# Queries from 256 on: decay rows fetched two heads ahead into five zeroed buffers, not one head ahead into three

## The chip, the cores and the metric

One core of a Trainium2 chip runs the whole program. The metric is the device time of one execution in microseconds (us); lower is better. Engines are called TensorE (PE; its weight loads are PEld), VectorE (DVE), ScalarE (ACT), GpSimd (POOL) and SyncE (SP). SP issues nearly all transfers here, in the order of its queue.

## What is computed

A causal attention with per-step decay, then two MLP blocks. Four batches, eight heads, 576 positions, 64 channels per head. Only the attention's scores matter for the change:

```python
scores = scale * np.matmul(q, k.transpose(0, 1, 3, 2))
cum = np.cumsum(np.log(np.clip(f, 0.0001, 1.0)), axis=-1)
decay = cum[:, :, :, None] - cum[:, :, None, :]
scores = np.where(causal, -1000000000.0, scores + decay)
attn = softmax(scores)            # row maximum taken off first, 1e-9 in the sum
out = np.matmul(attn, v)
x = out of all heads side by side
x = x + relu(layernorm(x) * g @ w_ch1) @ w_ch2
...                               # then a gated MLP with a mix over positions
```

The decay is a difference of two sums, one of the query's position and one of the key's, so four extra rows under a head's 64 channels (sum and one, each in a high and a low part) let the score matmul add it.

## The kernel before

The positions of a batch are worked on in three kinds of blocks: the first 128, the next 128, and the queries from 256 on (320 of them, `QW`). Beside the attention blocks run the token blocks of the first MLP (`mlp`, L808): its two products, L858 into `ph` and L843 into `acc`, are most of TensorE's work and alternate with the attention's matmuls. ScalarE makes `hh` (L869) and VectorE `hl` (L873) from `ph`.

The change is in the third kind, `attention` (L567), which runs once per batch, so 32 heads in all. It goes over four pairs of heads. For each head `operands` (L325) builds the two matmul operands: the key and query columns come by a DMA into `qk` (L330); ScalarE rounds them into `x1` and the queries' upper part into `x2` (both through `copy`, L319); VectorE writes the rounding remainders (L341 into `x1`, L342 into `x2`). Rows 64 to 67 of `x2` hold the four decay rows, which a DMA of SP brings from `decay_d` in device memory (L338); the other rows from 64 on must be zero, so the `x2` tiles are not taken from a rotating pool but are three fixed tiles (`x2z`), zeroed once by GpSimd (L335) and used in turn. `qk` and `x1` have three buffers each as well (`BUFS`, L29).

`weights` (L345) then makes scores of one query block: a matmul with `x2` and one with `x1` (L359), masking with a row minimum on VectorE (L363), exponential on ScalarE (L367), probabilities in two halves (L319 and L380), and a transpose by DMA (L382). Query blocks 2 and 3 are done head by head, block 4 for both heads of a pair together, so that the `x1` and `x2` tiles of both heads of a pair come free when block 4's matmuls are done. `operands` of a head is written one head before that head's `weights`.

The order on each engine and queue is not the order of the text. The program's scheduler runs a model of the chip at compile time and puts an instruction into its engine's queue when the model finds it ready; among ready ones, what was written earlier goes first, except where an order is written out (`after`, `in_order`; the transposes among themselves are). On the chip each queue then runs in that fixed order, and an instruction that waits holds up those behind it.

After its attention a block is stored (L1343), normalised in place (`norm`, L754; the centring is L776) and handed to the MLP.

Of the kernel before, what the change touches and what calls it, by code (L numbers as in the profile page):

```python
# [7 lines left out]
F32R = mybir.dt.float32r  # L8
# [10 lines left out]
P = 128  # L19
B, H, S, D = 4, 8, 576, 64  # L20
# [5 lines left out]
TOK = 256  # L26
QW = S - 2 * P
SC = 2.0 ** 14
BUFS = dict(vr=1, vp=2, qk=3, x1=3, x2=3, PT=4, sd=3, st=6, P16=5, xt=1)  # L29
BUFS0 = dict(vr=1, qk=1, e=4, diag=2, PT=2, st=4)  # L30
BUFS1B = dict(vr=4, vp=4, qk=4, sd=4, P16=4, PT=3, st=8)
BUFS1 = dict(vr=3, vp=3, qk=3, sd=2, P16=2, PT=2, st=6)
# [43 lines left out]
def qtile(i):  # L76
    return i * P, min(S, (i + 1) * P)


def f32(ap):  # L80
    return ap.bitcast(F32)
# [7 lines left out]
class Kernel:  # L89
# [227 lines left out]
    def copy(self, e, out, in_, scale=1.0):  # L317
# [4 lines left out]
        else:  # L322
            self.nc.vector.tensor_scalar(out=out, in0=in_, scalar1=scale, scalar2=None, op0=ALU.mult)

    def operands(self, bh):  # L325

        nc, at = self.nc, self.at
        W, C = QW, QW + S
        qk = at.tile([P, C], F32, tag="qk", name="qk", bufs=BUFS["qk"])
        nc.sync.dma_start(out=qk, in_=self.qk[bh // H, bh % H])  # L330
        x1 = at.tile([P, C], F32R, tag="x1", name="x1", bufs=BUFS["x1"])
        if not self.x2z:
            for i in range(BUFS["x2"]):
                self.x2z.append(at.tile([P, C], F32R, name=f"x2z{i}"))
                nc.gpsimd.memset(f32(self.x2z[i][64:]), 0.0)  # L335
        x2 = self.x2z[0]
        self.x2z.append(self.x2z.pop(0))
        nc.sync.dma_start(out=f32(x2[64:68]), in_=self.decay_d[:, bh // (2 * H) * 2 * H + bh % H * 2 + bh // H % 2])  # L338
        self.copy(0, x1, qk)
        self.copy(0, x2[:64, :W], qk[:64, :W])  # L340
        nc.vector.tensor_tensor(out=x1[64:, :W], in0=qk[64:, :W], in1=f32(x1[64:, :W]), op=ALU.subtract)  # L341
        nc.vector.tensor_tensor(out=x2[:64, W:], in0=qk[:64, W:], in1=f32(x1[:64, W:]), op=ALU.subtract)  # L342
        return [(x[:, :W], x[:, W:]) for x in (x2, x1)]

    def weights(self, i, heads):  # L345

        nc, at, bufs, q0 = self.nc, self.at, BUFS, 2 * P
        lo, hi = qtile(i)
# [218 lines left out]
    def attention(self, b, xT, xt):  # L567
        nc, at, bufs = self.nc, self.at, BUFS
        q0, W = 2 * P, QW
        stored = xt is None  # L570
        if stored:
            xt = at.tile([P, NP, S - 512], F32, tag="xt", name="xt", bufs=bufs["xt"])

        def values(p, vp, vsc, heads, behind=None):

            pav = self.bank("av")
            for kt in range(5):
                n0 = max(kt * P, q0) - q0
                for vi, pi in ((0, 1), (1, 0), (0, 0)):
                    for u in range(2):  # L580
                        us = slice(64 * u, 64 * u + 64)
                        ins = nc.tensor.matmul(  # L582
                            pav[us, n0:W], lhsT=vp[:, vi, kt, us], rhs=heads[u][1][:, 2 * kt + pi, n0:W],
                            start=(kt == 0 and (vi, pi) == (0, 1)), stop=(kt == 4 and (vi, pi) == (0, 0)), skip_group_check=True)
                        if behind is not None and kt == 0 and (vi, pi) == (0, 1):
                            self.after(ins, behind)
            nc.scalar.activation(xT[:, p, :], pav[:, :TOK], AF.Copy, scale=vsc)
            nc.scalar.activation(xt[:, p, :], pav[:, TOK:W], AF.Copy, scale=vsc)
            if p == 1:
                self.xs = self.mo_sum(xT)  # L590
            elif p == 2:
                nc.vector.tensor_tensor(out=self.xs, in0=self.xs, in1=xT[:, 2, :], op=ALU.add)

        late = None
        passes = self.operands(b * H)
        for p in range(NP):
            heads = []
            for u in range(2):
                heads.append((passes, at.tile([P, 10, W], F16, tag="PT", name="PT", bufs=bufs["PT"])))
                if 2 * p + u + 1 < H:  # L600
                    passes = self.operands(b * H + 2 * p + u + 1)
                if u:
                    vr = at.tile([P, 5, P], F32, tag="vr", name="vr", bufs=bufs["vr"])
                    nc.sync.dma_start(out=vr, in_=self.v[b, :, p * P : (p + 1) * P].rearrange("(t p) d -> p t d", p=P))
                yield
                for i in (2, 3):
                    done = self.weights(i, heads[u:])
                    if late and (u, i) == (1, 2):
                        yield
                        values(*late, done)  # L610
                    yield
            vp = at.tile([P, 2, 5, P], F16, tag="vp", name="vp", bufs=bufs["vp"])
            self.weights(4, heads)
            vsc = self.parts16(vr, vp[:, 0], vp[:, 1], b)
            late = p, vp, vsc, heads
            yield
        yield
        values(*late)
        yield
        if stored:  # L620
            nc.sync.dma_start(out=self.xt_d[:, :, b, :], in_=xt)
        return self.xs
# [907 lines left out]
```

## Time and profile before

| | us |
|---|---|
| three runs | 769.38, 771.96, 771.42 |
| median | 771.42 |
| the profiled execution | 774.42 |
| its span, first to last instruction | 772.6 |

Rows are of that one profiled execution. Times start with the span's first instruction. In a list of instructions the columns are start, duration, engine, line, operation, what is written and read, shapes and count; in brackets stands how long the engine was idle before, and what ended it. SPq is SP's queue of transfers.

### The profile page before, as it was taken

How to read it: one execution, taken by the hardware profiler on the slowest of the kernel's cores; microseconds unless marked ns; L12 is line 12 of the kernel's file. 1: busy time of each engine (PE TensorE's matmuls, PEld its weight loads, DVE VectorE, ACT ScalarE, POOL GpSimd, SP SyncE). 2: the span in 40 equal slices, each digit the busy share in tenths (PEclk: the TensorE clock that was granted, in tenths of full speed). 3: DMA queues.
4: the chain of work that ended last, by engine and by line, in shares of the span. 5: the costliest groups of instructions: out<-in, count | busy, mean ns of one | idle time of the engine just before them, and what ended most of it. 6: DMA issues, size and time to landing. Idle time of an engine off the chain costs nothing.

```text
span 772.6 us, 16271 instructions
## 1 busy us (share of the span) xinstructions
PE 747.0 (97%) x5924; PEld 573.0 (74%) x5924; DVE 584.9 (76%) x1549; ACT 528.1 (68%) x1318; POOL 67.2 (9%) x102
## 2 busy tenths in 40 slices
PE   8899998999998999999999999999999999999998
PEld 7788887888876787877878888644447668768676
DVE  7999799576589679979958964779534697785854
ACT  6898599576689588888958853477335765755633
POOL 6001101013101001101200200200012000000000
PEclk9999999999999899999999999999999999999999
DMA  8978793377589799997974874741015230000101
GB/s 264 296 255 295 242 215 71 73 180 124 171 160 170 186 183 174 198 215 159 200 184 102 127 112 143 197 153 56 1 20 110 70 97 28 31 32 1 62 2 62
DMA packets 164099, 104.68 MB, mean 135 GB/s; under 512 B 106146, under 2 KB 151298, under 8 KB 164020
## 3 DMA queue, kind: packets, MB, share of 16 engines
q1 hardware_dynamic: 157784, 96.60, 50.5%
q0 software_dynamic: 5376, 5.54, 5.6%
q10 hardware_dynamic: 860, 1.52, 0.6%
q8 instruction: 46, 0.75, 0.4%
q14 instruction: 33, 0.27, 0.1%
HBM read 64.37 MB, written 15.11 MB: 103 GB/s over the span
## 4 chain that ended last, share of the span: by engine, by line
PE 65%; DVE 13%; ACT 9%; DMA 8%; issue 3%; SPq 1%; DVEq 0%; ACTq 0%
PE ph L858 16%; PE acc L843 13%; PE pb L802 8%; PE pb L803 8%; PE pb L804 8%; PE s L359 3%; PE av L582 2%; DMA vr<-in_v_dram 2%; DMA raw<-in_moe_w_ch_dram 2%; PE s L843 2%; DVE wt L741 1%; DMA raw<-in_moe_w_in_dram 1%; DMA x2z<-decay_d 1%; DVE P L380 1%; ACT P L319 1%
## 5 line engine op out<-in xcount | busy, mean ns | idle before, releaser
L843 PE MATMUL acc<-hh,wt 128*128 128x256 f16 (+2 forms) x960 | 197.6, 296 | 3.0 <-ACT hh L869 2.9
L858 PE MATMUL ph<-xh,wt 128*128 128x256 f16 (+1 forms) x896 | 186.8, 290 | 4.2 <-DVE hl L873 4.1
L858 PEld LDWEIGHTS <-wt 128*128 128x128 f16 x1344 | 127.5, 99 | 50.3 <-issue 12.7
L843 PEld LDWEIGHTS <-wt 128*128 128x128 f16 x1344 | 129.0, 98 | 44.3 <-issue 5.8
L858 PE MATMUL ph<-xl,wt 128*128 128x256 f16 (+1 forms) x448 | 129.6, 289 | 0.0
L843 PE MATMUL acc<-hl,wt 128*128 128x256 f16 (+1 forms) x416 | 116.1, 283 | 0.6 <-DVE hl L873 0.6
L869 ACT ACTIVATE hh<-ph 128x256 f16<-128x256 f32 (+2 forms) x128 | 50.8, 397 | 55.7 <-PE ph L858 55.4
L873 DVE SCALAR_TENSOR_TENSOR hl<-ph,hh 128x256 f16<-128x256 f32 (+1 forms) x112 | 50.7, 454 | 42.2 <-ACT hh L869 41.8
L319 ACT ACTIVATE P<-sd,st 128x512 f16<-128x512 f32 (+1 forms) x128 | 70.0, 585 | 8.5 <-DVE st L370 5.2
L380 DVE SCALAR_TENSOR_TENSOR P<-sd,st,P 128x384 f16<-128x384 f32 (+1 forms) x96 | 58.6, 631 | 11.1 <-ACT P L319 10.2
L367 ACT ACTIVATE sd<-sd,st 128x384 f32<-128x384 f32 (+2 forms) x80 | 54.5, 682 | 13.3 <-DVE st L363 13.1
L359 PE MATMUL s<-x2z 128*128 128x384 f32 (+3 forms) x128 | 48.6, 388 | 6.1 <-DMA x2z<-decay_d 4.2
L363 DVE CUSTOM_DVE_ANT_0 sd<-s,mask 128x384 f32<-128x384 f32 (+2 forms) x80 | 46.0, 580 | 4.7 <-PE s L359 4.0
L894 POOL DMA_DIRECT2D x_d<-t x36 | 32.0, 1042 | 194.0 <-DVE t L890 162.3
L359 PE MATMUL s<-x 128*128 128x384 f32 (+3 forms) x128 | 42.4, 340 | 0.0
L804 PE MATMUL pb<-wsh,vh 128*128 128x288 f16 x128 | 36.6, 286 | 0.0
L803 PE MATMUL pb<-wsl,vh 128*128 128x288 f16 x128 | 36.6, 286 | 0.0
L802 PE MATMUL pb<-wsh,vl 128*128 128x288 f16 x128 | 36.6, 286 | 0.0
L804 PE MATMUL pb<-gh,woh 128*128 128x288 f16 x128 | 35.0, 286 | 0.0
L803 PE MATMUL pb<-gl,woh 128*128 128x288 f16 x128 | 34.9, 286 | 0.0
L802 PE MATMUL pb<-gh,wol 128*128 128x288 f16 x128 | 33.3, 286 | 0.0
L916 ACT ACTIVATE gh<-u 128x288 f16<-128x288 f32 x32 | 14.0, 438 | 26.6 <-DVE u L1255 25.4
(332 smaller groups left out, 1691.7 us busy)
## 6 DMA issues: line engine op xcount, KB each, us to landing
raw<-in_moe_w_ch_dram SPq DMA_DIRECT2D x32, 512.0 KB
qk<-in_qk_dram SPq DMA_DIRECT2D x32, 448.0 KB
vraw<-in_v_dram SPq DMA_DIRECT2D x5, 1024.0 KB
vr<-in_v_dram SPq DMA_DIRECT2D x16, 320.0 KB
x_d<-xT SPq DMA_DIRECT2D x9, 512.0 KB
x_d<-t POOLq DMA_DIRECT2D x36, 128.0 KB, 4.3
out_dram<-o SPq DMA_DIRECT2D x32, 144.0 KB
raw<-in_moe_w_in_dram SPq DMA_DIRECT2D x8, 512.0 KB
```

Of the source, the lines that this page charges most:

```text
L319: self.nc.scalar.activation(out, in_, AF.Copy, scale=scale)
L359: nc.tensor.matmul(ps[: R * u + R, : c1 - c0], lhsT=x[:, lo - q0 - R * u : hi - q0], rhs=y[:, c0:c1], start=g == 0, stop=g == len(heads[u] ...
L363: nc.vector.tensor_tensor_reduce(out=sd[:M, c0:c1], in0=ps[:M, : c1 - c0], in1=mask, scale=-0.125, scalar=3e38 if n == 0 else st[:M, n - 1 ...
L367: nc.scalar.activation(sd[:M, :N], sd[:M, :N], AF.Exp, bias=st[:M, n : n + 1], scale=-1.0, accum_out=st[:M, 2:3])
L380: low = nc.vector.scalar_tensor_tensor(out=dl, in0=src, scalar=rs, in1=dh, op0=ALU.mult, op1=ALU.subtract)
L802: first = mm(out, lhsT=al, rhs=bh, start=start, stop=False, **kw)
L803: mm(out, lhsT=ah, rhs=bl, start=False, stop=False, **kw)
L804: mm(out, lhsT=ah, rhs=bh, start=False, stop=stop, **kw)
L843: ins = nc.tensor.matmul(acc[m], lhsT=a, rhs=b, start=bank not in clear, stop=last and e == len(terms) - 1, skip_group_check=True)
L858: ins = nc.tensor.matmul(ph, lhsT=a, rhs=b, start=k == e == 0, stop=k == NK - 1 and e == len(terms) - 1)
L869: relu = nc.scalar.activation(hh, ph, AF.Relu)
L873: nc.vector.scalar_tensor_tensor(out=hl, in0=ph, scalar=0.0, in1=hh, op0=ALU.max, op1=ALU.subtract)
```

## The change

A new function `decay_rows` takes the decay rows' DMA, and the zeroed tiles with their memsets, out of `operands`. `attention` calls it for heads 0 and 1 of a batch before the first `operands`, and then for head h+2 just ahead of the call of `operands` for head h+1. The tiles go into a list, `ready`, from which `operands` takes the oldest. There are five zeroed tiles, not three.

```diff
-BUFS = dict(vr=1, vp=2, qk=3, x1=3, x2=3, PT=4, sd=3, st=6, P16=5, xt=1)
+BUFS = dict(vr=1, vp=2, qk=3, x1=3, x2=5, PT=4, sd=3, st=6, P16=5, xt=1)
...
+    def decay_rows(self, bh):
+
+        if not self.x2z:
+            for i in range(BUFS["x2"]):
+                self.x2z.append(self.at.tile([P, QW + S], F32R, name=f"x2z{i}"))
+                self.nc.gpsimd.memset(f32(self.x2z[i][64:]), 0.0)
+        x2 = self.x2z[0]
+        self.x2z.append(self.x2z.pop(0))
+        self.nc.sync.dma_start(out=f32(x2[64:68]), in_=self.decay_d[:, bh // (2 * H) * 2 * H + bh % H * 2 + bh // H % 2])
+        self.ready.append(x2)
+
     def operands(self, bh):
...
-        if not self.x2z:
-            for i in range(BUFS["x2"]):
-                self.x2z.append(at.tile([P, C], F32R, name=f"x2z{i}"))
-                nc.gpsimd.memset(f32(self.x2z[i][64:]), 0.0)
-        x2 = self.x2z[0]
-        self.x2z.append(self.x2z.pop(0))
-        nc.sync.dma_start(out=f32(x2[64:68]), in_=self.decay_d[:, bh // (2 * H) * 2 * H + bh % H * 2 + bh // H % 2])
+        x2 = self.ready.pop(0)
...
         late = None
+        self.ready = []
+        for u in range(2):
+            self.decay_rows(b * H + u)
         passes = self.operands(b * H)
...
+                if 2 * p + u + 2 < H:
+                    self.decay_rows(b * H + 2 * p + u + 2)
                 if 2 * p + u + 1 < H:
                     passes = self.operands(b * H + 2 * p + u + 1)
```

## Rows read from the trace of the kernel before

**Rows 1.** The page, first part: busy time, share of the span, instructions.
```profile
PE 747.0 (97%) x5924; PEld 573.0 (74%) x5924; DVE 584.9 (76%) x1549; ACT 528.1 (68%) x1318; POOL 67.2 (9%) x102
```

**Rows 2.** Stretches: length, busy by PE, PEld, DVE, ACT, POOL; clock, DMA share, GB/s.
```profile
205.00:470.00 265.00, 255.16 (x2323) 211.33 (x2322) 215.95 (x586) 206.96 (x537) 25.68 (x40) 0.98 0.83 165
240.00:260.00 20.00, 16.68 (x133) 13.41 (x132) 14.54 (x41) 12.85 (x36) 3.40 (x6) 0.83 1.08 195
290.00:300.00 10.00, 8.10 (x52) 5.79 (x50) 9.77 (x27) 8.72 (x20) 2.15 (x3) 0.83 0.79 187
470.00:612.00 142.00, 141.53 (x871) 83.06 (x869) 88.54 (x212) 78.92 (x170) 12.04 (x14) 1.00 0.38 99
```

**Rows 3.** Waits, 205 to 470 us: who for whom; us in total, times, longest.
```profile
PE s L359 <- DMA x2z<-decay_d: 4.2, 2, 3.3
...
PE s L359 <- DVE st L363: 1.9, 1, 1.9
```

**Rows 4.** Chain of waits, 240 to 260 us: start, duration, what.
```profile
244.71 6.26 DMA x2z<-decay_d
...
251.11 1.83 PE s L359 x4
```

**Rows 5.** Timeline of SP's queue, 226 to 252 us.
```profile
234.86 7.00 SPq L382 DMA_TRANSPOSE PT<-P  x4
...
242.59 2.03 SPq L382 DMA_TRANSPOSE PT<-P  x1
244.71 1.38 SPq L338 DMA_DIRECT2D x2z<-decay_d  x2
```

**Rows 6.** Timelines of TensorE, VectorE and ScalarE, 245 to 257 us.
```profile
247.40 0.40 PE L359 MATMUL s<-x 128*128 128x512 f32 x1
251.11 0.66 PE L359 MATMUL s<-x2z 128*128 128x384 f32 x1 [3.32 <-DMA x2z<-decay_d]
...
256.18 0.50 PE L858 MATMUL ph<-xh,wt 128*128 128x256 f16 x2
256.51 0.27 PE L858 MATMUL ph<-xl,wt 128*128 128x256 f16 x1
...
245.61 0.75 DVE L342 TENSOR_TENSOR x2z<-qk,x 64x576 fp32r<-64x576 f32 x1
...
248.48 0.41 DVE L873 SCALAR_TENSOR_TENSOR hl<-ph,hh 128x256 f16<-128x256 f32 x1
...
252.92 0.61 DVE L380 SCALAR_TENSOR_TENSOR P<-sd,st,P 128x384 f16<-128x384 f32 x1
...
249.88 2.08 ACT L319 ACTIVATE P<-sd,st 128x512 f16<-128x512 f32 x4
256.93 0.38 ACT L869 ACTIVATE hh<-ph 128x256 f16<-128x256 f32 x1 [4.98 <-PE ph L858]
```

**Rows 7.** SP's own waits, 205 to 470 us: us in total, times, longest.
```profile
SPq L338 <- PE s L359: 6.0, 5, 4.6
```

**Rows 8.** Chain of waits, 350 to 362 us.
```profile
357.19 2.28 DMA x2z<-decay_d
...
359.60 1.05 PE s L359 x4
```

**Rows 9.** Timeline of all engines, 352 to 366 us.
```profile
357.31 0.75 DVE L342 TENSOR_TENSOR x2z<-qk,x 64x576 fp32r<-64x576 f32 x1
...
359.60 0.41 PE L359 MATMUL s<-x2z 128*128 128x384 f32 x1 [0.86 <-DMA x2z<-decay_d]
```

**Rows 10.** Instructions of tile x2z: count, ns (least/median/most), first and last start.
```profile
L359 PE MATMUL s<-x2z x128: 288/391/660, 204.9 to 455.6; 128*128 128x384 f32 x32, 128*128 128x512 f32 x32, 128*128 128x288 f32 x32, 128*64 128x288 f32 x32
...
L335 POOL MEMSET x2z<- x3: 839/839/841, 188.1 to 189.7; 64x896 f32 x3
```

**Rows 11.** Timelines of VectorE and TensorE, 286 to 297 us.
```profile
289.73 1.42 DVE L776 TENSOR_TENSOR xT<-xT,av 128x256 f32<-128x256 f32 x4 [2.21 <-DMA x_d<-xT]
...
292.48 0.46 PE L359 MATMUL s<-x2z 128*128 128x384 f32 x1 [1.90 <-DVE st L363]
```

## The prediction

> **What bounds the kernel now.** I read the page first: TensorE is busy 97% of the span [rows 1], so a stall elsewhere costs nothing unless it reaches TensorE. Then the table by stretch, for the stage that the change touches, the attention of queries from 256 on (205 to 470 us). There TensorE is busy 255.16 of 265.00 us, so 9.8 us are idle, and its granted clock is 0.98; all of the lost clock sits in two short stretches around 250 and 295 us with 0.83 each [rows 2]. Behind the stage TensorE is busy 141.53 of 142.00 us [rows 2]: what the stage gives back moves the rest forward and isn't swallowed there. Then the list of waits of that stage, to see who makes TensorE idle: 4.2 of the 9.8 us, in two places, are score matmuls (L359) that wait for the landing of decay rows; 1.9 us, in one place, wait for the masking on VectorE [rows 3]. Last the chain of waits and the timeline around each place.
>
> The first place decides. The decay rows of two heads are issued at 244.71 us, right behind a transpose that held SP from 242.59 on, and the first lands 6.26 us later [rows 4, 5]. TensorE issued its last matmul before it at 247.40 (0.40 us long) and stands from 247.80 to 251.11 us, the 3.32 us of the row [rows 6]. Everything else that this matmul needs is there: its head's correction (L342) ended at 245.61 + 0.75 = 246.36 [rows 6]. While TensorE stands, its clock falls to the lower level, 1.2 GHz, and it is back at 2.4 GHz at 256.5 us: the pair of L858 matmuls at 256.18 still took 0.50 us, the one at 256.51 took 0.27 [rows 6].
>
> Why the rows come so late: there are three zeroed buffers. A pair of heads gives two of them back when its last scores (third query block) are done, so the rows of an odd head can be asked for only then, one odd head ahead of their use. In SP's list of waits the row DMAs stand 6.0 us in five places for score matmuls [rows 7].
>
> **The change, part by part.** *Rows earlier.* With five buffers, head h takes the buffer of head h-5, whose scores were done one or two pairs ago. For the head that stalls, that buffer has been free since before the four transposes which SP issues from 234.86 to 241.86 us [rows 5]. The scheduler puts an instruction into a queue when its own model finds it ready, so I take the issue to move ahead of 234.86, at least 244.71 - 234.86 = 9.9 us earlier. Even a landing of 6.26 us then ends by 241.1, and TensorE comes at 247.80. The wait is gone, not merely shorter.
>
> *What is late next, first place.* TensorE goes on at 247.80; four score matmuls take 1.05 us at the upper clock [rows 8], to 248.85. The second MLP product behind them needs at the latest the hl that VectorE ends at 248.48 + 0.41 = 248.89 [rows 6]: 0.04 us. In the trace TensorE does these four from 251.11, at the lower level, in 1.83 us [rows 4]. So 251.11 - 247.80 = 3.3 us of idle time, and half of the slow time from 251.11 to 256.4, (256.4 - 251.1) / 2 = 2.65 us, come free: 5.95 us. ScalarE and VectorE must follow. ScalarE has queued probability scalings until 249.88 + 2.08 = 251.96, VectorE works until 252.92 + 0.61 = 253.53; after that ScalarE idles 4.98 us for TensorE (the row at 256.93) [rows 6]. With TensorE 6 us ahead, the next hh is ready to be read at about 251, so ScalarE starts it at 251.96 at the earliest, and VectorE its hl at 253.53. TensorE's next scores (the third query block of the pair) then wait for VectorE's masking until about 255.5, where TensorE by itself is there at 254.5 to 255. I take off 0.5 us: **5.45 us**.
>
> *Second place.* The row at 359.60 shows 0.86 us of idle time for rows that were issued at 357.19 and landed 2.28 us later [rows 8, 9]. The head's correction ended at 357.31 + 0.75 = 358.06, before TensorE stopped, at 359.60 - 0.86 = 358.74 [rows 9]. No clock was lost here. **0.7 us**, with 0.16 kept for what else is close.
>
> *Two more zeroed buffers.* Two more memsets on GpSimd at 0.84 us each, 1.7 us behind the three that start from 188.1 to 189.7 us; the first score matmul starts at 204.9 [rows 10]. They lie beside other work, and the first two buffers are zeroed first. If that cover were gone, the first rows of the stage would come 1.7 us later, with 14 us still in hand. Two buffers are 2 x 896 x 4 = 7168 bytes per partition; what shares that space changes, which no row prices. Bounds: 0 and the 1.7 us of the memsets; I take 0, since TensorE has MLP matmuls to do in that stretch.
>
> *The queues that the rows are moved past.* Each row DMA now stands ahead of transposes and key loads on SP. Their number stays 32, so SP's issue time is the same. A transpose that comes behind a pair of them is later by the pair's issue, 1.38 us at the costliest [rows 5]; but it was behind another pair before. Lower bound: the 6.0 us of SP standing for score matmuls go as well [rows 7], which lets transposes through sooner and could give up to the 1.9 us gap of VectorE's masking. Upper bound: one such gap more. I take 0.
>
> *Given back.* TensorE now runs 6 us ahead of the DMA queues, whose share in the stage is 0.83 and 1.08 around the stall [rows 2]. One stall that a transfer causes is still there: VectorE centres a block in place only when its store has landed, 2.21 us of waiting at 289.73, and TensorE stands 1.90 us at 292.48 [rows 11]. I let half of one more such gap come up: -1.0 us.
>
> **The sum.** 5.45 + 0.7 - 1.0 = 5.15 us. The profiled execution took 774.42 us (span 772.6 and 1.82 around it), which would become 769.3. The median of the three runs shown is 3.0 us below the profiled one; set against it, 771.42 - 5.15 = **766.3 us**, 0.7% faster. About 0.3% (2.3 us) is what a measurement of this kernel can tell from no change.
>
> **The rivals.** *A. The stall is the profiled execution's, or the rows don't move.* What speaks for it: the same transfer landed after 2.28 us in the other place [rows 8] and 6.26 us here [rows 4], and the timed runs are 3.0 us shorter than the profiled one. With 2.28 us the rows would land at 246.99, before TensorE asks at 247.80, and only the second place would pay, under 0.9 us. The same comes out if the scheduler's model leaves the row DMAs where they stand. Time: 771.4 - 0.7 = 770.7. Against it: the DMA engines are full there by the trace (share 1.08 [rows 2]), and the transposes that fill them run in every execution.
>
> The Trainium skill (DMA: Bandwidth & Descriptors, section Latency and other measured facts) has a fixed cost of about 2 us for a DMA, most of it the wait for memory, which it puts at 0.2 us on average and 2 us under load. By that figure 244.71 + 2 = 246.7 (an estimate), no stall, and the change would be worth nothing in the first place; the trace agrees at the second place (2.28 us) and not at the first (6.26 us).
>
> *B. New gaps in a new order: slower.* The order on every queue is dealt by the scheduler's model, and the freed buffers change what is ready when: ScalarE's copy into x2 no longer waits for the buffer, and transposes and loads on SP are sorted anew. The mechanism is the one at 289.73 [rows 11]: a store of a block lands late, VectorE stands in front of its centring with maskings queued behind, and TensorE stands for these. Price: 1.90 us idle and the lower clock behind it, (1 - 0.83) x 10 us = 1.7 us [rows 2], 3.6 us each. One such gap leaves 1.5 us of gain, two turn it into 2 x 3.6 - 5.15 = 2.1 us of loss, and three, 3 x 3.6 - 5.15, give 771.4 + 5.7 = 777.1. It decides from two on. For it: one such wait reaches TensorE already [rows 11]. Against it: the stores hang on the end of a block's attention, four times in the stage, and the change doesn't touch them.
>
> *C. More than the sum.* The gap at 292.48 goes as well, with its clock: 3.6 us more, 762.7 us. The transposes that come sooner speak for it; the store whose landing it hangs on is not touched.
>
> **How the numbers follow.** Forecast 0.45, C 0.13, A (with rows that don't move, and one new gap) 0.24, B 0.18. Faster by over 0.3%: 0.45 + 0.13 = 0.58; within: 0.24; slower: 0.18. The range goes from 762.0 (C and a little of the give-back) up to 774.0: it takes in A and the two-gap end of B (773.5) and leaves out B's three gaps.
>
> **What would show it.** Right: no score matmul that waits for the rows; SP's row DMAs ahead of the transposes by 10 us or more; a granted clock of 1.00 around 250 us; the stage shorter by about 5 us and everything behind it as long as before. Wrong: the rows earlier and TensorE idle at the same matmul for another releaser (VectorE's L342 or L363), a stage before 205 us that differs, or new stretches at the lower clock elsewhere.

## The result and the profile after

| | before | after |
|---|---|---|
| median, us | 771.31 (769.38 to 773.03, 6 runs) | 780.88 (779.14 to 786.29, 6 runs) |
| profiled execution, us | 774.42 | 786.29 |
| its span, us | 772.6 | 784.5 |

The ratio is 1.0133, 95% interval 1.0108 to 1.0158: the change costs 9.6 us. The forecast was 766.3 us in a range from 762.0 to 774.0, so it is wrong in its sign and outside its range. The profiled execution of after is the slowest of its six, 5.4 us over their median.

The page of the kernel after, engines' busy time; against [rows 1] TensorE's work is the same, its share smaller:

```profile
PE 748.1 (95%) x5924; PEld 572.3 (73%) x5924; DVE 585.8 (75%) x1549; ACT 528.7 (67%) x1318; POOL 69.0 (9%) x104
```

The kernel after, stretches (length, busy by PE, PEld, DVE, ACT, POOL; clock, DMA share, GB/s):

```profile
205.00:470.00 265.00, 246.50 (x2217) 202.55 (x2215) 215.19 (x581) 206.31 (x534) 25.85 (x40) 0.98 0.84 164
240.00:260.00 20.00, 18.27 (x153) 14.39 (x151) 16.14 (x46) 15.23 (x42) 3.06 (x5) 0.91 1.16 175
290.00:300.00 10.00, 9.06 (x74) 6.82 (x73) 8.38 (x23) 7.54 (x21) 1.17 (x3) 1.00 0.78 167
390.00:410.00 20.00, 14.65 (x140) 11.43 (x138) 7.72 (x19) 8.39 (x23) 0.20 (x1) 0.83 0.88 150
470.00:612.00 142.00, 140.94 (x860) 83.96 (x859) 86.43 (x201) 72.76 (x156) 12.06 (x14) 1.00 0.37 94
```

Against [rows 2] the two old places are better (TensorE 18.27 for 16.68 of 20 us, 9.06 for 8.10 of 10), and the stage as a whole is worse: 246.50 us busy for 255.16. A new stretch, 390 to 410 us, has 5.35 us of TensorE standing and a granted clock of 0.83. The clock of 1.00 around 250 us, a sign of being right in the prediction, did not come: it is 0.91 from 240 to 260 us, where TensorE now stands for a masking of VectorE:

```profile
242.83 0.40 PE L364 MATMUL s<-x2z 128*128 128x288 f32 x1 [1.73 <-DVE st L368]
```

The kernel after, waits from 205 to 470 us (who for whom; us in total, times, longest):

```profile
DVE P L385 <- ACT P L319: 19.6, 19, 5.3
ACT x2z L319 <- DMA qk<-in_qk_dram: 19.3, 9, 5.5
...
PE av L587 <- ACT hh L879: 5.3, 1, 5.3
PE s L364 <- DVE st L368: 4.0, 5, 1.7
...
PE av L587 <- DMA PT<-P: 3.0, 2, 2.2
```

The score matmuls' wait for decay rows [rows 3] is gone. A new one stands in the list: ScalarE's copy of the queries into `x2` waits in nine places, 19.3 us in all, for the landing of its head's keys. Before, that copy's waits were for score matmuls. VectorE's waits for ScalarE's probabilities are longer (19.6 us, before 10.2), and so are TensorE's for VectorE's masking (4.0 us in five places, before 1.9 in one [rows 3]). The row of before:

```profile
DVE P L380 <- ACT P L319: 10.2, 15, 1.5
```

What the longest of the nine places does, first on ScalarE's timeline, 392 to 403 us (start, duration, engine, line, operation; in brackets the idle time before):

```profile
392.12 0.72 ACT L319 ACTIVATE P<-sd,st 128x512 f16<-128x512 f32 x1 [0.26 <-DVE st L375]
398.32 0.47 ACT L319 ACTIVATE x2z<-qk 64x320 fp32r<-64x320 f32 x1 [5.48 <-DMA qk<-in_qk_dram]
398.69 0.94 ACT L319 ACTIVATE P<-sd,st 128x512 f16<-128x512 f32 x2
...
400.93 0.82 ACT L280 ACTIVATE vp<-vr,vsc 128x640 f16<-128x640 f32 x1
401.65 0.61 ACT L319 ACTIVATE P<-sd,st 128x384 f16<-128x384 f32 x1
402.15 0.65 ACT L879 ACTIVATE hh<-ph 128x256 f16<-128x256 f32 x2
```

The same place in the chain of waits:

```profile
392.29 6.00 DMA qk<-in_qk_dram
...
398.32 0.02 ACT x2z L319
...
402.26 0.56 ACT hh L879 x2
402.81 0.78 issue
403.59 0.45 PE av L587
```

And TensorE's timeline:

```profile
397.97 0.27 PE L853 MATMUL acc<-hh,wt 128*128 128x256 f16 x1
403.59 0.45 PE L587 MATMUL av<-PT,vp 128*64 128x320 f16 x1 [5.35 <-ACT hh L879]
...
404.16 0.63 PE L853 MATMUL acc<-hh,wt 128*128 128x256 f16 x2
```

The keys are issued at 392.29 and land 6.00 us later. ScalarE is free at 392.84 and stands in front of the copy until 398.32; the probabilities, the values' copy (`vp`) and `hh` are queued behind it. TensorE finishes its last work at 398.24 and stands 5.35 us until `vp` and `hh` are made; then pairs of L853 take 0.63 us at the lower clock level, 1.2 GHz. (It is the 29th head's copy, and that head's first score matmul comes at 439.70: the copy is not urgent, it is only in the way.) How the other eight reach TensorE was not followed one by one.

Why the copy stands there. Three `x1` and three `qk` buffers are as before. With five `x2` tiles head h takes the tile of head h-5. For an odd head 2p+1 that is head 2p-4, of pair p-2; for an even head 2p it is head 2p-5, of pair p-3, one pair earlier still. So an even head's copy into `x2` no longer waits for a tile; its keys are the last thing it lacks, and they are asked for only when head h-3 has given its `qk` back. The copies on ScalarE's timeline, before (no bracket: none waited for its keys):

```profile
243.60 0.46 ACT L319 ACTIVATE x2z<-qk 64x320 fp32r<-64x320 f32 x1
243.96 0.94 ACT L319 ACTIVATE x<-qk 128x896 fp32r<-128x896 f32 x1
244.80 0.46 ACT L319 ACTIVATE x2z<-qk 64x320 fp32r<-64x320 f32 x1
245.16 0.94 ACT L319 ACTIVATE x<-qk 128x896 fp32r<-128x896 f32 x1
```

and after, from there on:

```profile
248.12 0.95 ACT L319 ACTIVATE x<-qk 128x896 fp32r<-128x896 f32 x1 [1.60 <-PE s L364]
248.98 0.45 ACT L319 ACTIVATE x2z<-qk 64x320 fp32r<-64x320 f32 x1
249.34 0.93 ACT L319 ACTIVATE x<-qk 128x896 fp32r<-128x896 f32 x1
...
253.85 0.47 ACT L319 ACTIVATE x2z<-qk 64x320 fp32r<-64x320 f32 x1 [0.40 <-DMA qk<-in_qk_dram]
```

Before, four copies come in a row, when a pair has given its tiles back; the keys of these two heads had been issued at 220.10 and 232.33, over 12 us before. After, one copy in four, the even head's, comes alone right behind its keys (issued at 250.59 for the one at 253.85), and all nine that wait are of this kind. That the scheduler's model expects the landing sooner than the chip delivers is argued from this order, not measured.

### The profile page after: what moved, and what is told of

It is laid out like the page before. It is cut to its first block, busy times and chain, and to the rows that moved or that the text cites. A ratio compares the mean times of both kernels' runs of the same rounds, so it can differ in the third digit from the quotient of the medians.

```text
span 784.5 us, 16239 instructions
## 1 busy us (share of the span) xinstructions
PE 748.1 (95%) x5924; PEld 572.3 (73%) x5924; DVE 585.8 (75%) x1549; ACT 528.7 (67%) x1318; POOL 69.0 (9%) x104
## 4 chain that ended last, share of the span: by engine, by line
PE 55%; DVE 16%; DMA 13%; ACT 10%; issue 4%; SPq 1%; POOL 0%; ACTq 0%; DVEq 0%
PE ph L868 12%; PE acc L853 11%; PE pb L812 8%; PE pb L813 8%; PE pb L814 8%; DMA qk<-in_qk_dram 4%; PE s L364 2%; DMA vr<-in_v_dram 2%; DVE P L385 2%; PE av L587 2%; DMA raw<-in_moe_w_ch_dram 2%; PE s L853 1%; DMA PT<-P 1%; DVE wt L751 1%; ACT P L319 1%
## 5 line engine op out<-in xcount | busy, mean ns | idle before, releaser
L853 PE MATMUL acc<-hh,wt 128*128 128x256 f16 (+2 forms) x960 | 198.8, 296 | 4.8 <-ACT hh L879 3.3
L853 PEld LDWEIGHTS <-wt 128*128 128x128 f16 x1344 | 129.6, 99 | 46.2 <-issue 6.1
L853 PE MATMUL acc<-hl,wt 128*128 128x256 f16 (+1 forms) x416 | 116.3, 283 | 1.2 <-DVE hl L883 1.1
L319 ACT ACTIVATE P<-sd,st 128x512 f16<-128x512 f32 (+2 forms) x128 | 70.7, 585 | 8.8 <-DVE st L375 5.7
L385 DVE SCALAR_TENSOR_TENSOR P<-sd,st,P 128x384 f16<-128x384 f32 (+2 forms) x96 | 59.6, 639 | 20.9 <-ACT P L319 20.4
L587 PE MATMUL av<-PT,vp 128*64 128x320 f16 (+2 forms) x480 | 30.4, 273 | 9.0 <-ACT hh L879 5.3
L587 PEld LDWEIGHTS <-vp 128*64 128x64 f16 x480 | 24.4, 111 | 17.1 <-issue 14.0
```

The lines of the kernel that those rows point to most:

```text
L319: self.nc.scalar.activation(out, in_, AF.Copy, scale=scale)
L385: low = nc.vector.scalar_tensor_tensor(out=dl, in0=src, scalar=rs, in1=dh, op0=ALU.mult, op1=ALU.subtract)
L587: ins = nc.tensor.matmul(pav[us, n0:W], lhsT=vp[:, vi, kt, us], rhs=heads[u][1][:, 2 * kt + pi, n0:W], start=(kt == 0 and (vi, pi) == (0, ...
L853: ins = nc.tensor.matmul(acc[m], lhsT=a, rhs=b, start=bank not in clear, stop=last and e == len(terms) - 1, skip_group_check=True)
```

## The experiments

Theories: **S**, the five buffers set ScalarE in front of late keys, and that is the loss; **R**, the rows' transfers, earlier on SP, are the loss; **G**, removing the waits for rows gains nothing on its own, because another transfer is late right behind. Each program is dealt anew by the scheduler, so one run shows what it costs as a whole, not one instruction. The medians of before in the groups of runs were 771.2 (e1 to e4), 771.3 (e0, e5 to e7), 770.3 (e8, e9), 770.8 (e10) and 771.6 (e11).

### e0: the kernel before, profiled once more

> The kernel before once more, for a second profile of it. The prediction's sum needs the 3.3 us wait for decay rows around 250 us in every execution: then it stands here again at 3 us or more, with the lower clock behind it. Its rival A: the wait is under 1 us here and the execution about 3 us shorter than the first profiled one (771 instead of 774).

No edit; 772.68 us. Its waits, and its timeline of TensorE at the two places:

```profile
PE s L359 <- DMA x2z<-decay_d: 3.8, 2, 2.2
```
```profile
250.98 0.41 PE L359 MATMUL s<-x2z 128*128 128x384 f32 x1 [2.23 <-DMA x2z<-decay_d]
...
293.04 0.41 PE L359 MATMUL s<-x2z 128*128 128x384 f32 x1 [1.54 <-DMA x2z<-decay_d]
```

and its chain of waits at the first:

```profile
245.32 5.53 DMA x2z<-decay_d
```

Neither branch came as written. The first wait stands again, now 2.23 us, and costs no clock: the matmul takes 0.41 us, where it took 0.66 in [rows 6]. The rows' landing took 5.53 us. The second wait is at another matmul, at 293.04 us, and the one at 359.60 [rows 9] isn't there. So the first wait is the program's; the lower clock behind it, and the place of the second, changed from one execution to the other.

### e2: five buffers alone; e5: four alone

> The kernel before with five zeroed buffers and nothing else: the rows are asked for where they were written before. Theory 1: the buffers alone free the x2 copy, so 778 to 783 us and x2 copies that wait 15 to 20 us for keys. Rival 2 (fetching two heads ahead does it): 769 to 773. Rival 3: somewhere in 765 to 785.

> The kernel before with four zeroed buffers and nothing else. Theory (an even head's tile is freed one pair earlier by the fifth buffer only; with four no x2 copy stands for keys; where in the text the rows are fetched matters little, since readiness orders the queue): as the kernel with four buffers and rows two heads ahead, 770 to 774 us, no wait for decay rows. Rival (the call two heads ahead matters by itself): more than 3 us away from that kernel, or the waits for decay rows are back.

```diff
-BUFS = dict(vr=1, vp=2, qk=3, x1=3, x2=3, PT=4, sd=3, st=6, P16=5, xt=1)
+BUFS = dict(vr=1, vp=2, qk=3, x1=3, x2=5, PT=4, sd=3, st=6, P16=5, xt=1)
```

(e5: `x2=4`.) e2: 779.79 us (779.04 to 780.31, 4 runs), ratio 1.0103 (1.0072 to 1.0134). e5: 772.69 us (10 runs), 1.0011 (0.9983 to 1.0038). Waits of e2:

```profile
ACT x2z L319 <- DMA qk<-in_qk_dram: 14.1, 7, 3.3
...
PE av L582 <- ACT x2z L319: 2.4, 1, 2.4
```

e2 leaves the rows' DMA where before has it in the text, and loses 8.6 us with the same wait on ScalarE, again all at even heads. It has no gap as long as the 5.35 us of after; its longest on TensorE, 2.35 us, is put down to that copy. In both runs no score matmul waits for rows any more. The buffers do that; fetching two heads ahead isn't needed for it. For the same reason e2 does not tell S from R: the rows of the head that stalled in [rows 6] are issued at 232.12 in e2, at 231.57 in after and at 244.71 before. e7 below does.

### e3: the change with four buffers

> The changed kernel with four buffers. Head h takes the tile of head h-4, still two pairs back, so the x2 copy is free before the keys land. Theory 1: as the changed kernel, 777 to 783 us, with x2 copies waiting for keys 12 to 20 us. Rival 2: the same 777 to 783. Rival 3: differs from the changed kernel by several us either way.

```diff
-BUFS = dict(vr=1, vp=2, qk=3, x1=3, x2=5, PT=4, sd=3, st=6, P16=5, xt=1)
+BUFS = dict(vr=1, vp=2, qk=3, x1=3, x2=4, PT=4, sd=3, st=6, P16=5, xt=1)
```

772.40 us (768.41 to 775.32, 10 runs), 1.0004 (0.9979 to 1.0029): what I expected did not come, it is 8.5 us under after. With four tiles both heads of a pair take the tiles of pair p-2, and no copy into `x2` waits for keys. So the step from four buffers to five costs 8.5 us (after against e3), or 7.1 us with the rows' call as before (e2 against e5). It isn't faster than before either, with no wait for rows in it. TensorE's timeline of e3 in the stage has one long gap:

```profile
393.98 0.30 PE L587 MATMUL av<-PT,vp 128*64 128x320 f16 x1 [3.63 <-DMA PT<-P]
```

and SP's queue ahead of it:

```profile
383.58 2.06 SPq L341 DMA_DIRECT2D qk<-in_qk_dram  x2
385.76 1.24 SPq L387 DMA_TRANSPOSE PT<-P  x1
387.10 0.69 SPq L614 DMA_DIRECT2D vr<-in_v_dram  x1
388.24 4.91 SPq L387 DMA_TRANSPOSE PT<-P  x3
```

This is the value product of a block's last pair; its transposes are issued at 388.24, behind two key loads and a value load.

How much later the same matmul into `ph` (counted from the start) begins than in e0, the profiled execution nearest to before's median, in us:

| in e0 at | after | e3 | e7 | e9 | e11 |
|---|---|---|---|---|---|
| 203 us | 0.2 | 0.4 | 0.2 | 0.6 | 0.2 |
| 301 us | 4.4 | -2.7 | -0.2 | -2.2 | -4.5 |
| 327 us | 6.8 | -1.0 | 0.8 | -0.5 | -3.7 |
| 342 us | 2.0 | -5.0 | -0.7 | -4.5 | -7.1 |
| 390 us | 6.9 | -4.3 | -1.2 | -4.1 | -6.3 |
| 399 us | 13.4 | 0.5 | -1.2 | -6.8 | -7.2 |
| 471 us | 12.7 | 0.2 | -1.4 | -4.8 | -7.4 |

(All columns fall between 327 and 342 us because e0 lost time there, with TensorE's granted clock at 0.77, not because these kernels gained. A single value can also move because the order of TensorE's matmuls differs.) After loses 6.5 us of its 12.7 between 390 and 399 us, the place shown above; e3 loses 4.7 there, for its transposes. Behind the stage, at 560 us, each of these columns is within 1 us of its value at 471.

### e1 and e4: the copy into x2 ordered behind that into x1

> The changed kernel, but ScalarE's copy of the queries into x2 is written behind the same head's copy into x1, so it can't go ahead before x1's buffer is free. Theory 1 (the five buffers let the scheduler put the x2 copy right behind the modelled landing of the keys; on the chip the keys land later and ScalarE stands 19.3 us in nine places): no x2 copy waits for keys any more, the rows still come early, 766 to 773 us. Rival 2 (the rows that go ahead on SP delay transposes and key loads): still 779 to 783. Rival 3 (any new order of the queues or new places in SBUF cost this much): 775 to 785, with gaps in other places.

> The kernel before with the x2 copy written behind the x1 copy, three buffers. Control for e1: with three buffers both copies of an odd head are freed by the same scores, so little moves. Theory 1: 769 to 774 us, the two waits for decay rows (4.2 us) still there. Rival 3 (any new order costs): 775 to 785.

```diff
-            self.nc.scalar.activation(out, in_, AF.Copy, scale=scale)
+            return self.nc.scalar.activation(out, in_, AF.Copy, scale=scale)
...
-        self.copy(0, x1, qk)
-        self.copy(0, x2[:64, :W], qk[:64, :W])
+        first = self.copy(0, x1, qk)
+        self.after(self.copy(0, x2[:64, :W], qk[:64, :W]), first)
```

e1 (on after): 774.79 us (772.47 to 776.57, 10 runs), 1.0027 (1.0000 to 1.0054). e4 (the same on before): 775.45 us (10 runs), 1.0053 (1.0027 to 1.0079), where I had expected 769 to 774; of the two waits for rows one is left, 1.1 us. In e1 no copy into `x2` waits for keys, and it is 6.1 us under after, though not within the 766 to 773 that S asked for. But the order by itself costs 4.2 us in before (e4), so this edit is no clean measure, and e7 was made for that. Waits of e1:

```profile
PE av L587 <- DMA PT<-P: 6.2, 3, 4.6
```

4.55 us of it stand at 394.02, again the last pair's value product.

### e7: the change as it is, the even heads' copy on GpSimd

> The changed kernel (five buffers), but an even head's copy into x2 is made by GpSimd, not ScalarE. Theory 1 (it is ScalarE standing in front of late keys that costs): ScalarE stands for keys under 4 us instead of 19, GpSimd stands instead, 770 to 776 us. Rival (five buffers cost by something else: places in SBUF, SP's order): 779 to 783 us.

```diff
-        self.copy(0, x2[:64, :W], qk[:64, :W])
+        self.copy(1 if bh % 2 == 0 else 0, x2[:64, :W], qk[:64, :W])
```

772.52 us (768.15 to 774.59, 10 runs), 1.0009 (0.9983 to 1.0036), 8.4 us under after, with five buffers and the rows two heads ahead. Its waits:

```profile
POOL x2z L321 <- DMA qk<-in_qk_dram: 84.2, 12, 12.7
```

GpSimd now stands for the keys, 84.2 us (idle time, counted from the end of its work before), and no wait of TensorE in the stage is put down to it; it is busy for 37.22 of the 265 us of the stage. S is shown as far as such a run can: early copies and late keys stay, the engine that stands in front is another, and 8.4 of the 9.6 us are back. R falls here: the rows are as early as in after (230.96 for the head that stalled), and the other rival of this run, the places in SBUF, falls with it, since the five tiles are those of after. VectorE's waits for ScalarE's probabilities are back at 10.5 us. One thing is not kept apart: ScalarE also has 16 copies of 0.45 to 0.47 us less to do. And a new order alone can cost 4.2 us (e4); but the kernels sort by the wait: after and e2, which have it, take 780.9 and 779.8 us, and e1, e3, e5 and e7, which don't, 772.4 to 774.8.

### e6, e8, e9, e10: the last pair's value product later

> Rows two heads ahead with four buffers, and the last pair's product with the values of batches 0 to 2 written four steps of the attention later (about one step of the MLP), so that MLP matmuls stand in front of it. Theory (what the rows give by 390 us, 4 to 7 us, is given back at one place near 394 us, where TensorE waits for the transposes of a batch's last pair): the wait there is under 1.5 us and the time 764 to 769 us. Rival (the stage is bound elsewhere, the wait comes back at another place): 771 to 776 us.

> As the kernel with late values (four buffers, rows two heads ahead, last pair's product four steps later), and that product is also ordered behind the last probability half (L380 of the kernel before) that VectorE has been given by then, the next batch's. In the run with late values the order had hardly moved: TensorE still stood 2.9 us near 392 us for the transposes of a batch's last pair. Theory (this one wait gives back what the rows gain): the wait is gone or under 1 us, and the time 764 to 768.5 us, 0.4 to 0.9% under the kernel before. Rival (the stage is bound by its transfers and by VectorE, the wait comes back elsewhere): 769 to 774 us.

> The same with six steps in place of four. Theory: as with four, 764 to 769 us. Rival: 769 to 775 us, with waits for transposes or stores elsewhere.

> Control for the run with six steps: the kernel before (three buffers, rows one head ahead) with the same later, ordered product of a batch's last pair. If the rows earlier are worth something once nothing gives it back, the waits for decay rows (2 to 5 us in all) stand here and the time is 769 to 772 us, 1.5 to 3.5 us over that run. Rival (the later product alone made it faster): 766.5 to 768.5 us.

To G: what remains once S is gone is no gain at all (e3, e5, e7). On e3's kernel the product of a batch's last pair (not the last batch's) was put some steps of the schedule later (e6: 4), and also ordered behind the last probability half of the pair (e8: 4, e9: 6). `xt` gets a second buffer for it, and the loads from `xt_d` move behind its stores. e10 is the control: e9's edit on before, with three buffers and rows one head ahead.

```diff
+LATE, LATEB = 6, (0, 1, 2)
...
+        self.lastlow = low
...
-        yield
-        values(*late)
+        for _ in range(1 + (LATE if b in LATEB else 0)):
+            yield
+        values(*late, self.lastlow if b < B - 1 else None)
```

| | us | ratio (95%) | TensorE's wait for these transposes |
|---|---|---|---|
| e6 | 769.98 (769.08 to 774.64, 10) | 0.9991 (0.9966 to 1.0015) | 2.92 at 392.23 |
| e8 | 770.99 (767.99 to 774.47, 12) | 1.0003 (0.9977 to 1.0029) | 2.43 at 392.35 |
| e9 | 767.91 (765.86 to 770.10, 12) | 0.9960 (0.9939 to 0.9981) | none there |
| e10 | 768.14 (766.39 to 772.96, 12) | 0.9968 (0.9947 to 0.9990) | none there |

e6 and e8 missed what they were for: the wait stayed above 1.5 us. In e9 it is gone. Stretches of e3:

```profile
385.00:400.00 15.00, 11.37 (x97) 8.72 (x95) 4.42 (x13) 3.80 (x11) 0.00 (x0) 0.89 0.70 143
```

and of e9:

```profile
205.00:470.00 265.00, 258.25 (x2386) 215.68 (x2384) 222.21 (x599) 210.22 (x545) 25.68 (x40) 1.00 0.88 173
385.00:400.00 15.00, 14.88 (x142) 12.55 (x141) 7.46 (x18) 6.48 (x18) 0.20 (x1) 1.00 0.81 183
```

e9 is faster than both kernels, by 2.4 us against before. But so is e10, whose profile still has a wait for rows:

```profile
PE s L360 <- DMA x2z<-decay_d: 2.6, 1, 2.6
```

So the later product makes this gain; the rows and a fourth buffer on top add nothing that can be told (767.9 and 768.1). That wait was seen in e10's slowest execution of twelve (772.96 us); whether the others have it isn't known. G's place is real, but removing it doesn't bring the rows' gain out.

### e11: before without the rows' transfers

> The kernel before without the DMA of the decay rows in the attention of queries from 256 on: these rows stay zero, so the decay is left out of these scores; all else is as before, three buffers included. It prices the waits for the rows in timed executions, with the buffers' order kept. The prediction's sum: 3.5 to 6 us under the kernel before, 765 to 768. If the rows' waits cost little outside the first profile, or are given back at the end of a batch: 769.5 to 772 us.

```diff
-        nc.sync.dma_start(out=f32(x2[64:68]), in_=self.decay_d[:, bh // (2 * H) * 2 * H + bh % H * 2 + bh // H % 2])
```

Without these 32 transfers the decay is left out of the scores from query 256 on. 765.55 us (764.13 to 768.86, 6 runs) against 771.59, 0.9924 (0.9899 to 0.9949): 6.0 us less. Stretch of e11:

```profile
205.00:470.00 265.00, 260.25 (x2396) 217.75 (x2394) 219.34 (x599) 211.20 (x547) 25.84 (x40) 1.00 0.89 173
```

A program without waits for rows and with no other loss in their place is thus 6 us faster. The run also takes 32 transfers off SP and the DMA engines and is dealt anew, so the 6.0 us are not the waits alone.

## Why the prediction was wrong, point by point

**Rows earlier: right.** No score matmul waits for rows. The head that stalled in [rows 6] has its rows issued at 231.57, 13.1 us earlier than in [rows 5], where at least 9.9 were forecast. The wait is gone, not moved to another releaser of that matmul. SP's timeline of after:

```profile
231.57 0.77 SPq L333 DMA_DIRECT2D x2z<-decay_d  x2
```

**What the waits are worth: not contradicted, and not settled.** 5.45 + 0.7 us were claimed. e11, with all else that it removes, gives 6.0. Of the 5.45, 2.65 us were a clock loss that e0's first place didn't have; its two waits are 3.8 us together. The 0.7 us of the second place, at 359.60, were not there in e0 at all. The sum took the savings of one execution, the dearer of the two, off the median.

**Two more zeroed buffers: the step that failed.** It priced the memsets (0 to 1.7 us), left the space without a price, and took 0. A buffer is also a permission: every instruction that had waited for it is ready earlier. Here that is ScalarE's copy of every even head. The measured term is 7.1 to 8.5 us (e2 against e5, after against e3), and taking ScalarE from in front of the keys gives back 8.4 us (after against e7). In before the wait for a tile had kept the copy out of the queue until the keys were in, as far as the order of the copies shows. The working asked what each moved DMA is moved past on SP and GpSimd and didn't ask it of ScalarE, the engine whose instruction the freed tile lets go first; nor did it work out by pair which head's tile comes free when. It wrote that the scores of head h-5 were done one or two pairs ago; it is two pairs back for an odd head and three for an even one, and that odd step of the fifth buffer is what lets the copy go ahead.

**Rival B had the place and the wrong price.** It said that the copy no longer waits for its buffer, and then priced VectorE's centring behind a store [rows 11], at 3.6 us a gap, 18%. The range's upper end of 774.0 left out three such gaps, 777.1; the loss is larger still, 9.6 us.

**Given back, 1.0 us: too small.** With ScalarE's part gone (e3, e5, e7) nothing that can be measured is left of the gain. In e3 4.7 us go at one place, at the last pair's value product; I had looked for the give-back at the stores. e1 stands there too, and e7 doesn't; where e7 loses its gain is open. In e5's profiled execution the stage is 3.8 us shorter than in e0's (2.3 us behind it at 203 us, 1.5 ahead at 471); but it had fallen behind by 2.5 us between 82 and 127 us, and the lead goes between 505 and 525 us, both outside the stage in which the `x2` tiles are used. Whether other executions of e5 do the same isn't known. Why e9 with early rows equals e10 without is open too.

**Rival A fell.** The first wait and its long landing repeat (6.26, then 5.53 us), and the rows did move. The Trainium skill (DMA: Bandwidth & Descriptors, section Latency and other measured facts) has a fixed cost of about 2 us for a DMA; the second profile of before disagrees with it at this place (5.53 us) as the first did.

**Behind the stage: right.** From 470 us the lag of after stays within 1 us (12.7 at 471, 13.6 at 560).

**GpSimd's memsets and SP's queue: right or harmless.** The last of five memsets starts at 192.3, and the first score matmul at 205.8 waits for none. SP still stands 6.8 us for score matmuls in front of the rows' DMA, where 6.0 stood [rows 7]: the forecast's lower bound, that this goes, did not come.

## What to carry to other kernels

Before adding a buffer, list every instruction that the buffer's reuse had held back, on every engine, and ask of each what it waits for next and what stands behind it in its in-order queue: a buffer too few can be the cover of a late transfer. Work out for each n which iteration's release frees the tile (here n = 4 takes both heads of a pair back to the same pair, 3 and 5 don't), and try n and n+1. An early step that nobody needs soon belongs on the engine on which nothing urgent is queued, and a stall should be priced from more than one profiled execution.

## What the runs showed of the hardware

I had not expected how far a load's landing spreads. The same 14 KB row transfer landed 2.28 us after its issue in one place of before [rows 8] and 6.26 us (5.53 in e0) in another. Both stand right behind transposes in SP's queue, the second by [rows 5] and the first behind this row of it; the DMA share was 0.81 around the first (355 to 360 us) and 1.18 around the second (243 to 251 us). A head's keys (448 KB) took 6.00 us at 392.29, where the DMA share from 390 to 410 us is 0.88.

```profile
349.12 7.97 SPq L382 DMA_TRANSPOSE PT<-P  x6
```

Nor had I expected how cheap standing is on the right engine: with 84.2 us of GpSimd waiting for keys the time can't be told from before's (e7), and with 19.3 us of ScalarE waiting for the same heads' keys it is 8.4 us longer (after).
